# Chunk log sums by VectorE transposes instead of one-column matmuls in a fused gated-linear-attention and squared-ReLU kernel, with the last output tile evicted in halves

## The chip, the cores and the metric

The kernel runs on one core of one Trainium2 chip. The metric is device time in microseconds (us), the median of several runs. Engine names are those of the profile: PE is TensorE (PEld its weight loads), DVE is VectorE, ACT is ScalarE, POOL is GpSimd, SP is SyncE, which issues the DMAs.

## The reference

Two stages. The first is a recurrence over 768 steps for 4 batches x 8 heads with head size 48; its result is the input of a two-layer block with a squared ReLU.

```python
# q, k, v, alpha: (4, 8, 768, 48), alpha in 0.8 to 1.0
for t in range(S):
    state = alpha[:, :, t, :, None] * state + einsum('bhd,bhe->bhde', k[:, :, t], v[:, :, t])
    y[:, :, t] = einsum('bhd,bhde->bhe', q[:, :, t], state)
x = y.transpose(0, 2, 1, 3).reshape(3072, 384)
out = square(maximum(x @ w_in, 0)) @ w_out      # w_in 384 x 2048, w_out 2048 x 384
```

## The kernel before

**Chunks.** The 3072 tokens are 24 chunks of 128 tokens, six to a batch (`NCH = 6`). The recurrence is done chunk by chunk in matrix form. For a chunk, `at` (alpha) is loaded and ScalarE takes its logarithm into `L_s`. A step called `p0` on TensorE multiplies `L_s` by an upper triangle of ones (`utri_b`): its 384 columns are the cumulative log sums of all rows, in the PSUM bank `pm`. Four more matmuls of `p0`, one for each pair of heads, have `L_s` as weights and a single column of ones: they give the sum over the whole chunk with the head's channel on the partition, four columns more in the same bank. From `pm` ScalarE reads `A` = exp, `Ainv` = exp(-), and the two halves of `ae_s` = exp of the chunk sums (L421 to L431). VectorE makes `qA_s = q * A` (L440) and `kI_s = k * Ainv` (L443); TensorE transposes both (`p1q`, `p1k`), VectorE copies them out as `qkT` (L367), and so on: scores `sc`, masked scores `sm` (L504), the state update `st` (matmul, then VectorE's `st * ae_s`, L538, then ScalarE's copy `sb`), the chunk's output `py` (steps `p3a`, `p3b`), its copy `xn`, its transpose (`p4`) and the copy into `xT_big`. `p0`, `p1`, `p4` and others take one of two PSUM banks (`GLA_BANKS`) in turn. Chunks 0 to 3 are handled as two double chunks in another layout (`add_super`); from chunk 8 on, chunks go in pairs, so a pair has an even and an odd chunk. The ones-column form of `p0` serves every chunk from 4 to 23.

**The block.** `add_moe1` multiplies `xT_big` by `w_in` (three matmuls of 256 or 128 or 512 columns to a piece, then ScalarE's relu `r`, L790, and VectorE's square into `gT`, L798). `add_moe2` multiplies `gT` by `w_out` (16 matmuls of 384 columns to a token tile), ScalarE or VectorE copies the PSUM bank to `ob` (L828, L830), and SP issues one DMA of 192 KB to the output (L837).

**What sets the order.** All work is entered as `Op`s with an engine, a guessed duration, dependences and a priority. `Plan.run` is a list scheduler in Python: it places every op by these guesses, and then emits all ops in the order of their planned starts. The engines therefore run a written-out order; each engine works strictly in that order, and what the guesses miss becomes a wait on the chip. The guesses include `LD` (us for one load of a chunk's tensor, 1.05) and `OUT_LATE = 3.5` (an output DMA's planned start is that much later than its eviction). `gate` lets a chunk's `p0` start only when it is at most 3.5 chunks ahead of the block. The framework below adds the semaphore waits for data and for shared buffers, PSUM banks among them.

Of the kernel before, what the change touches and what calls it, by code (L numbers as in the profile page):

```python
# [8 lines left out]
FP32 = mybir.dt.float32  # L9
BF16 = mybir.dt.bfloat16  # L10
AF = mybir.ActivationFunctionType
# [45 lines left out]
def after(op, x=0.0):  # L57
    return (op, x)
# [86 lines left out]
def kernel(  # L145
# [10 lines left out]
    nc = tc.nc  # L156
    B, H, S, D = q.shape
    HD = H * D
    P = 128
    DP = 64  # L160
    NP = H // 2
    NCH = S // P
    d_model, d_ff = moe_w_in.shape
# [3 lines left out]
    NT = n_tok // P  # L167
# [5 lines left out]
    out_r = out.rearrange("(tt p) n -> tt p n", p=P)  # L173
# [73 lines left out]
    def pin(ins):  # L247
        tc.keep_in_program_order(ins)

    def mm(*a, **kw):  # L250
        pin(nc.tensor.matmul(*a, **kw))  # L251
# [14 lines left out]
    def psum(op, shape, dt):  # L266
        i = op.slot.bank
        return banks[i].tile(shape, dt, name=f"bank{i}")
    X_SLACK = 0.2
    LD = 1.05  # L270
    LD2 = 1.51
    WLD = 2.05
    SQ_PRIO = 0.0
# [1 line left out]
    def add(eng, dur, emit, *deps, **kw):  # L275
        return plan.add(Op(eng, dur, emit, deps, **kw))
# [46 lines left out]
    state = {}  # L323
    SRC = dict(srcs)
    EARLY = 2 * 3
    PAIRS = 8
    LEAD = 3.5

    NS = 2
    SIDE = 1  # L330
    EITHER, SLOW = {"DVE": 0.47, "POOL": 0.95}, {"POOL": 0.95}
    KI_ON = [[EITHER, EITHER], [EITHER, EITHER]]
# [59 lines left out]
    def add_chunk(s):  # L392
        d = C[s]
        b, c = divmod(s, NCH)
        i = s % NBUF
        L, qA, kI, ae = L_s[:, i], qA_s[:, i], kI_s[:, i], ae_s[:, i]
        old = C[s - NBUF].get("end") if s >= NBUF else None
        g = dict(prio=-10.0 + s * 0.01)
        last = c == NCH - 1

        def e_ln():
            pin(nc.scalar.activation(L[:, :, 0:D], d["at"], AF.Ln))  # L402
        ln = d["use_at"] = add("ACT", 0.41, e_ln, d["ld_at"], old, prio=-15.0 if s < EARLY else -5.0)

        def e_vb():
            d["vb"] = work.tile([P, H, D], BF16, name="vb", bufs=4)
            pin(nc.gpsimd.tensor_copy(d["vb"], d["vt"]))  # L407
        vb = d["use_vt"] = add("POOL", 0.55, e_vb, d["ld_vt"], old, prio=-5.0)

        def e_p0():  # L410
            pm = d["pm"] = psum(p0, [P, 512], FP32)
            mm(pm[:, 0:HD], lhsT=utri_b[:, 0, :], rhs=L[:, :, 0:D], start=True, stop=True)
            for p in range(NP):
                mm(pm[:, HD + p:HD + p + 1], lhsT=L[:, 2 * p:2 * p + 2, :], rhs=ones_col,
                   start=True, stop=True)
        p0 = Op("PE", 0.27, e_p0, [ln], takes=GLA_BANKS, lat=0.17, **g)
        p0.gla = s

        def e_A():
            d["A"] = work.tile([P, H, D], BF16, name="A")  # L420
            pin(nc.scalar.activation(d["A"], d["pm"][:, 0:HD].rearrange("p (h d) -> p h d", h=H), AF.Exp))  # L421

        def e_Ai():
            d["Ai"] = work.tile([P, H, D], BF16, name="Ainv")
            pin(nc.scalar.activation(d["Ai"], d["pm"][:, 0:HD].rearrange("p (h d) -> p h d", h=H), AF.Exp, scale=-1.0))  # L425

        def e_ae0():
            pin(nc.scalar.activation(ae[0:64, :, 0], d["pm"][0:64, HD:HD + NP], AF.Exp))

        def e_ae1():  # L430
            pin(nc.scalar.activation(ae[64:128, :, 1], d["pm"][64:128, HD:HD + NP], AF.Exp))  # L431
        plan.add(p0)
        a_ = add("ACT", 0.38, e_A, p0, **g)
        ai = add("ACT", 0.38, e_Ai, p0, after(a_), **g)
        ae0 = add("ACT", 0.18, e_ae0, p0, after(ai), **g)
        ae1 = add("ACT", 0.19, e_ae1, p0, after(ae0), **g)
        p0.gives = ae1

        def e_qA():
            pin(nc.vector.tensor_mul(qA[:, :, 0:D], d["qt"], d["A"]))  # L440

        def e_kI():
            pin(nc.vector.tensor_mul(kI[:, :, 0:D], d["kt"], d["Ai"]))  # L443
        mq = d["use_qt"] = add("DVE", 0.47, e_qA, a_, d["ld_qt"], old, **g)
        mk = d["use_kt"] = add("DVE", 0.47, e_kI, ai, d["ld_kt"], old, **g)

        def e_p1q():
            d["pT"] = psum(p1q, [P, 2 * NP, P], BF16)
            for p in range(NP):
                tr(d["pT"][:, p, :], qA[:, 2 * p:2 * p + 2, :], ident_bf)  # L450

        def e_p1k():
            for p in range(NP):
                tr(d["pT"][:, NP + p, :], kI[:, 2 * p:2 * p + 2, :], ident_bf)
        p1q = plan.add(Op("PE", 0.22, e_p1q, [mq], takes=GLA_BANKS, **g))
        p1k = plan.add(Op("PE", 0.22, e_p1k, [mk, after(p1q)], lat=0.15, **g))

        def e_cp(lo, hi):
            if lo == 0:
                d["qkT"] = work.tile([P, 2 * NP, P], BF16, name="qkT")  # L460
            cast(cpk if lo else cp, d["qkT"][:, lo:hi, :], d["pT"][:, lo:hi, :])
        if s < EARLY:
            cp = add({"ACT": 0.49, "DVE": 0.34}, 0, lambda: e_cp(0, NP), p1q, **g)
            cpk = add({"DVE": 0.34, "ACT": 0.49}, 0, lambda: e_cp(NP, 2 * NP), p1k, after(cp, -9.0), **g)
        else:
            cp = cpk = add("DVE", 0.61, lambda: e_cp(0, 2 * NP), p1k, **g)
        p1q.gives = cpk

        d.update(cps=[cp, cpk], mk=mk, vb_op=vb, ae1=ae1, kI=kI, ae=ae)
        if s < PAIRS:  # L470
            add_scores(s, 1)
            add_back(s)
        elif s % 2:
            add_scores(s - 1, 2)
            add_back(s - 1)
            add_back(s)
# [90 lines left out]
    def add_super(u):  # L567
# [135 lines left out]
        for ab in any_:  # L703
            s = 2 * u + ab
            c = pair[ab]
            r = slice(HF * ab, HF * ab + HF)
            before = C[s - 1].get("sb") if s else None
            if s < NCH - 1:
                def e_ps(c=c, r=r, s=s):
                    if s == 0:  # L710
                        state["ps"] = ps_st.tile([P, NP, 2 * D], FP32, name="st")
                    st = c["st"] = state["ps"]
                    for t in any_:
                        for p in range(NP):
                            mm(st[:, p, :], lhsT=kI[r, t, 2 * p:2 * p + 2, :], rhs=d["vb"][t][r, 2 * p:2 * p + 2, :],
                               start=(s == 0 and t == 0 and p == 0), stop=True, skip_group_check=True)
                ps = plan.add(Op("PE", 0.35, e_ps, [*mk, *vb, ae1, before], lat=0.16, **g))

                def e_stm(c=c, ab=ab):
                    st4 = c["st"].rearrange("p n (j e) -> p n j e", j=2)  # L720
                    pin(nc.vector.tensor_mul(st4, st4, bcast(ae[:, ab], D)))  # L721
                stm = add("DVE", 0.47, e_stm, ps, ae1, prio=ST_PRIO)

                def e_sb(c=c):
                    c["sbt"] = work.tile([P, NP, 2 * D], BF16, name="sb")
                    pin(nc.scalar.copy(c["sbt"], c["st"]))
                c["sb"] = add("ACT", 0.37, e_sb, stm, prio=-12.0)

            def e_p3a(c=c, r=r, s=s, ab=ab):
                c["py"] = psum(c["p3a"], [P, 512], FP32)  # L730
                for p in range(NP):
                    mm(c["py"][:, 2 * p * D:2 * (p + 1) * D], lhsT=d["qT"][:, p, ab].rearrange("k t c -> k (t c)"), rhs=C[s - 1]["sbt"][:, p, :],
                       start=(p == 0), stop=False, skip_group_check=True)

            def e_p3b(c=c, r=r, s=s):
                if s == 0:
                    c["py"] = psum(c["p3b"], [P, 512], FP32)
                for x in any_:
                    for hh in range(2):
                        for p in range(NP):  # L740
                            h = 2 * p + hh
                            mm(c["py"][:, h * D:(h + 1) * D], lhsT=d["sm"][x][r, hh, p, :], rhs=d["vb"][x][r, h, :],
                               start=(s == 0 and x == 0 and hh == 0 and p == 0), stop=(x == 1), skip_group_check=True)
            p3a = None
            if s:
                p3a = c["p3a"] = plan.add(Op("PE", 0.2, e_p3a, [cq, before], takes=SUP_BANKS, **g))
            p3b = c["p3b"] = plan.add(Op("PE", 0.5, e_p3b, [*sm, *vb, after(p3a)], takes=None if s else SUP_BANKS,
                                         lat=0.15, **g))
            add_tail(s, p3b, p3a or p3b, g)

    GN = [4, 1, 1, 2, 2, 2, 2, 2, 2, 2, 2, 2]
    assert sum(GN) == NT
# [52 lines left out]
    def add_moe2(g, tt, before, box, quarters, pools):  # L805

        for qd in quarters:
# [12 lines left out]
            op.lat = 0.05  # L820
            before = op
        if quarters[-1] < NQ - 1:
            return op

        def e_ev():
# [113 lines left out]
```

## Time and profile before

| | |
|---|---|
| time, median of 3 runs | 189.08 us (188.58 to 189.12) |
| the profiled execution: its own time, its span | 187.66 us, 185.9 us |
| PE busy | 178.4 us, 96% of the span, granted clock 0.999 |
| DVE busy | 133.8 us (72%) |
| ACT busy | 122.6 us (66%) |
| POOL busy | 29.6 us (16%) |
| DMA, all of it from SP's queue but instruction loads | 29.89 MB, mean 163 GB/s |
| matmuls with the column of ones | 80, 4.8 us of overlapping durations |
| `ae_s` from PSUM, ScalarE | 2 x 20, 172 and 170 ns each |

A matmul's duration in the trace contains its way through the array, so that the next one starts long before it ends: what TensorE spends on it is the distance between starts. The same holds, less strongly, for VectorE and ScalarE back to back. "Idle before" of a group is the time that its engine stood idle just ahead of it, and the engine named behind it is the one whose semaphore ended that.

### The profile page before, as it was taken

To read this page: it belongs to the slowest core of one execution; us is meant where nothing else is said; L and a number is where in the kernel's file an instruction comes from. 1 tells how busy PE (TensorE), PEld (TensorE's weight loads), DVE (VectorE), ACT (ScalarE), POOL (GpSimd) and SP (SyncE) were. 2 spreads that over 40 slices of the span, in tenths; PEclk is the share of its full clock that TensorE was granted. 3 is DMA by queue.
4 is the path that set the end of the run, shared out by engine and by line. 5 is a ranking of instruction groups with operands and counts; after the bars stand their busy time and mean duration, and the time that the engine had idled before them with its cause. 6 is when DMAs were issued, how large, how long until landed. Compare 5 with 4: busy or idle time off the path is not lost.

```text
span 185.9 us, 5105 instructions
## 1 busy us (share of the span) xinstructions
PE 178.4 (96%) x2037; PEld 134.1 (72%) x2037; DVE 133.8 (72%) x280; ACT 122.6 (66%) x282; POOL 29.6 (16%) x47
## 2 busy tenths in 40 slices
PE   6889899999999999999999999999999999999992
PEld 2666684667887878878878878777868778767761
DVE  7688679875999986876976966866987976842400
ACT  3577779455896896776676776667778668434621
POOL 5044777411012111111020020020020000000000
PEclk9999999999999999999999999999999999999999
DMA  5999999899899999999997984691011011011112
GB/s 146 261 280 339 385 370 331 175 223 205 161 206 209 236 199 231 184 231 201 189 222 162 216 166 101 157 212 61 0 42 46 2 48 42 4 42 42 46 43 84
DMA packets 99176, 30.22 MB, mean 163 GB/s; under 512 B 92112, under 2 KB 98000, under 8 KB 99152
## 3 DMA queue, kind: packets, MB, share of 16 engines
q1 hardware_dynamic: 99152, 29.89, 68.1%
q8 instruction: 16, 0.26, 0.5%
q14 instruction: 8, 0.07, 0.1%
HBM read 25.17 MB, written 4.72 MB: 161 GB/s over the span
## 4 chain that ended last, share of the span: by engine, by line
PE 88%; DMA 3%; ACT 3%; SPq 2%; DVE 1%; issue 0%
PE bank L251 77%; PE bank L254 7%; DMA at<-in_alpha_dram 3%; PE sc L251 2%; PE st L251 2%; SPq L360 2%; DVE qkT L367 1%; ACT raw L691 1%; ACT L_s L579 0%; DVE qA_s L627 0%; ACT w_in_b L304 0%; DVE st L721 0%; ACT r L790 0%; ACT ob L830 0%; ACT A L610 0%
## 5 line engine op out<-in xcount | busy, mean ns | idle before, releaser
L251 PE MATMUL bank<-xT_big,w_in_b 128*128 128x256 bf16 (+2 forms) x600 | 73.1, 269 | 0.0
L251 PE MATMUL bank<-w_out_b,gT 128*128 128x384 bf16 x384 | 72.4, 326 | 0.0
L790 ACT ACTIVATE r<-bank 128x512 bf16<-128x512 f32 x96 | 56.9, 602 | 18.8 <-PE bank L251 16.5
L251 PEld LDWEIGHTS <-w_in_b 128*128 128x128 bf16 x600 | 52.5, 98 | 9.2
L798 DVE TENSOR_TENSOR gT<-r 128x512 bf16<-128x512 bf16 x96 | 45.2, 493 | 17.1 <-ACT r L790 16.6
L251 PEld LDWEIGHTS <-gT 128*128 128x128 bf16 x384 | 35.1, 97 | 17.8
L407 POOL CAST vb<-vt 128x384 bf16<-128x384 f32 x20 | 10.9, 550 | 92.7 <-PE bank L251 45.6
L367 DVE COPY qkT<-bank 128x1024 bf16<-128x1024 bf16 (+1 forms) x26 | 16.5, 649 | 6.3 <-PE bank L254 6.2
L830 ACT COPY ob<-bank 128x384 f32<-128x384 f32 x20 | 9.6, 479 | 14.6 <-PE bank L251 14.6
L504 DVE TENSOR_TENSOR sm<-sc,utri_b 128x512 bf16<-128x512 f32 x24 | 15.4, 684 | 2.0 <-PE sc L251 2.0
L365 ACT CAST xn<-bank 128x384 bf16<-128x384 f32 x24 | 10.9, 481 | 5.8 <-PE bank L251 5.7
L440 DVE TENSOR_TENSOR qA_s<-qt,A 128x384 bf16<-128x384 f32 x20 | 11.5, 577 | 3.8 <-ACT A L421 3.7
L251 PEld LDWEIGHTS <-qkT 64*128 64x128 bf16 (+2 forms) x304 | 10.4, 98 | 4.9 <-issue 2.5
L421 ACT ACTIVATE A<-bank 128x384 bf16<-128x384 f32 x20 | 9.9, 494 | 6.2 <-PE bank L251 6.2
L367 DVE COPY xT_big<-bank 128x384 bf16<-128x384 bf16 x21 | 7.4, 354 | 8.3 <-PE bank L254 8.2
L443 DVE TENSOR_TENSOR kI_s<-kt,Ainv 128x384 bf16<-128x384 f32 x20 | 11.3, 567 | 0.0
L543 ACT CAST sb<-st 128x384 bf16<-128x384 f32 x16 | 7.6, 476 | 5.2 <-DVE st L538 5.2
L402 ACT ACTIVATE L_s<-at 128x384 bf16<-128x384 f32 x20 | 10.0, 520 | 0.5 <-DMA at<-in_alpha_dram 0.4
L504 DVE TENSOR_TENSOR sm<-bank,utri_b 128x512 bf16<-128x512 f32 x16 | 10.2, 681 | 0.0
L251 PE MATMUL bank<-warm 128*128 128x256 bf16 (+1 forms) x41 | 8.2, 333 | 2.0 <-DVE both L216 1.3
L425 ACT ACTIVATE Ainv<-bank 128x384 bf16<-128x384 f32 x20 | 9.9, 496 | 0.0
L251 PE MATMUL bank<-vb,sm 128*128 128x48 bf16 (+1 forms) x224 | 9.6, 183 | 0.0
(70 smaller groups left out, 176.3 us busy)
## 6 DMA issues: line engine op xcount, KB each, us to landing
at<-in_alpha_dram SPq DMA_DIRECT2D x20, 192.0 KB, 3.9
qt<-in_q_dram SPq DMA_DIRECT2D x20, 192.0 KB, 3.7
kt<-in_k_dram SPq DMA_DIRECT2D x20, 192.0 KB, 4.0
vt<-in_v_dram SPq DMA_DIRECT2D x20, 192.0 KB, 3.7
out_dram<-ob SPq DMA_DIRECT2D x20, 192.0 KB, 2.3
wo<-in_moe_w_out_dram SPq DMA_DIRECT2D x4, 768.0 KB, 6.8
wi<-in_moe_w_in_dram SPq DMA_DIRECT2D x3, 768.0 KB, 8.0
at<-in_alpha_dram SPq DMA_DIRECT2D x2, 384.0 KB, 4.9
```

The source lines that it names most:

```text
L251: pin(nc.tensor.matmul(*a, **kw))
L254: pin(nc.tensor.transpose(*a))
L365: pin(nc.scalar.copy(out_t, in_t))
L367: pin(nc.vector.tensor_copy(out_t, in_t))
L402: pin(nc.scalar.activation(L[:, :, 0:D], d["at"], AF.Ln))
L407: pin(nc.gpsimd.tensor_copy(d["vb"], d["vt"]))
L421: pin(nc.scalar.activation(d["A"], d["pm"][:, 0:HD].rearrange("p (h d) -> p h d", h=H), AF.Exp))
L440: pin(nc.vector.tensor_mul(qA[:, :, 0:D], d["qt"], d["A"]))
L443: pin(nc.vector.tensor_mul(kI[:, :, 0:D], d["kt"], d["Ai"]))
L504: pin(nc.vector.tensor_mul(d["sm"][:, hh], d["sc"][hh], utri_b.to_broadcast([P, NP, P])))
L790: pin(nc.scalar.activation(box["r"][:, 0:w], box["ph"][:, 0:w], AF.Relu))
L798: pin(nc.vector.tensor_mul(gT[g][:, f0:f0 + per, lo * P:lo * P + n], r, r))
```

## The change

- From chunk 12 on (`TURN = 12`), `p0` keeps its 384-column matmul and loses the four one-column ones. VectorE instead transposes, in 32 x 32 blocks, the last 32 rows of the cumulative sums (partitions 96 to 127 of `pm`, where row 127 holds the chunk's sums): two instructions for a chunk, for channels 0 to 31 and for 16 to 47 of each of the eight heads, into a tile `tot`. ScalarE's `ae_s` is then made by four small exponentials that read column 31 of the blocks in `tot`, instead of two that read `pm`. The bank is given back, in the planner, after `Ainv` and the second transpose.
- The last token tile's eviction is split: VectorE copies 192 columns and SP issues their DMA, ScalarE copies the other 192 and issues their DMA itself. This SP issue has no `OUT_LATE`.
- `LD`, the planner's guess for a load, goes from 1.05 to 0.97.
- In the double chunks, `p3b` of both chunks is entered after the loop over them, and chunk 0's PSUM bank is taken by a planner-only op. `JOIN` keeps one `p3b` to a chunk.

```diff
-    LD = 1.05
+    LD = 0.97
...
+    TURN = 12
...
+    JOIN = [[(0,), (1,)], [(0,), (1,)]]
...
             mm(pm[:, 0:HD], lhsT=utri_b[:, 0, :], rhs=L[:, :, 0:D], start=True, stop=True)
-            for p in range(NP):
+            for p in range(NP if s < TURN else 0):
                 mm(pm[:, HD + p:HD + p + 1], lhsT=L[:, 2 * p:2 * p + 2, :], rhs=ones_col,
                    start=True, stop=True)
-        p0 = Op("PE", 0.27, e_p0, [ln], takes=GLA_BANKS, lat=0.17, **g)
+        p0 = Op("PE", 0.27 if s < TURN else 0.17, e_p0, [ln], takes=GLA_BANKS, lat=0.17, **g)
...
-        ae0 = add("ACT", 0.18, e_ae0, p0, after(ai), **g)
-        ae1 = add("ACT", 0.19, e_ae1, p0, after(ae0), **g)
-        p0.gives = ae1
+        Q = P - 32
+
+        def e_turn(w):
+            if w == 0:
+                d["tot"] = work.tile([P, 2, H, 32], FP32, name="tot", bufs=2)
+            pm = d["pm"][Q:P, 32 * w:32 * w + 1]
+            src = bass.AP(tensor=pm.tensor, offset=pm.offset, ap=[pm.ap[0], [D, H], [0 if w else 16, 2], [1, 16]])
+            pin(nc.vector.transpose(d["tot"][Q:P, w], src))
+
+        def e_aet(j, w):
+            n = 16 if w else 32
+            o = HF * j + 32 * w
+            src = d["tot"][Q:Q + n, w, :, 31].rearrange("p (n a) -> p a n", a=2)[:, j]
+            pin(nc.scalar.activation(ae[o:o + n, :, j], src, AF.Exp))
+        if s < TURN:
+            ae0 = add("ACT", 0.18, e_ae0, p0, after(ai), **g)
+            ae1 = add("ACT", 0.19, e_ae1, p0, after(ae0), **g)
+            p0.gives = ae1
+        else:
+            turn = add("DVE", 0.34, lambda: e_turn(0), p0, **g)
+            turn = add("DVE", 0.34, lambda: e_turn(1), p0, after(turn), **g)
+            ae1 = ai
+            for j in range(2):
+                for w in range(2):
+                    ae1 = add("ACT", 0.18, lambda j=j, w=w: e_aet(j, w), turn, after(ae1), **g)
+            fin = add("NIL", 0.0, lambda: None, ai, turn, lat=0.0, **g)
+            p0.gives = fin
...
             if s:
-                p3a = c["p3a"] = plan.add(Op("PE", 0.2, e_p3a, [cq, before], takes=SUP_BANKS, **g))
-            p3b = c["p3b"] = plan.add(Op("PE", 0.5, e_p3b, [*sm, *vb, after(p3a)], takes=None if s else SUP_BANKS,
-                                         lat=0.15, **g))
-            add_tail(s, p3b, p3a or p3b, g)
+                c["hold"] = plan.add(Op("PE", 0.2, e_p3a, [cq, before], takes=SUP_BANKS, **g))
+            else:
+                c["hold"] = plan.add(Op("NIL", 0.0, e_hold, sm, takes=SUP_BANKS, lat=0.0, **g))
...
+        for abs_ in JOIN[u]:
+            p3b = plan.add(Op("PE", 0.5 + 0.1 * len(abs_) - 0.1, lambda abs_=abs_: e_p3b(abs_),
+                              [*sm, *vb, *[pair[ab]["hold"] for ab in abs_]], lat=0.15, **g))
+            for ab in abs_:
+                add_tail(2 * u + ab, p3b, pair[ab]["hold"], g)
...
+        half = d_model // 2
+        if GT[g] + tt == NT - 1:
+            def e_evh(i):
+                if "ob" not in box:
+                    box["ob"] = opool.tile([P, 2, half], FP32, name="ob2", tag="ob")
+                cast(evs[i], box["ob"][:, i], box["po"][:, i * half:(i + 1) * half])
+
+            def e_outh(i):
+                pin((nc.sync, nc.scalar)[i].dma_start(out=out_r[NT - 1, :, i * half:(i + 1) * half], in_=box["ob"][:, i]))
+            evs = []
+            for i, e in enumerate(("DVE", "ACT")):
+                evs.append(add(e, 0.28, lambda i=i: e_evh(i), op, prio=-15.0))
+            add("OUT", 0.3, lambda: e_outh(0), evs[0], at=0.0)
+            add("ACT", 0.3, lambda: e_outh(1), evs[1])
+            box["first"].gives = evs[1]
+            return op
```

More of the change, by code (lines that the diff above doesn't have):

```diff
@@ L729, in e_p3a @@
             def e_p3a(c=c, r=r, s=s, ab=ab):
-                c["py"] = psum(c["p3a"], [P, 512], FP32)
+                c["py"] = psum(c["hold"], [P, 512], FP32)
                 for p in range(NP):
@@ L733, in e_p3a, with e_hold, e_p3b @@
                        start=(p == 0), stop=False, skip_group_check=True)
[L735 to L744, printed above, removed]
-            if s:
-                p3a = c["p3a"] = plan.add(Op("PE", 0.2, e_p3a, [cq, before], takes=SUP_BANKS, **g))
-            p3b = c["p3b"] = plan.add(Op("PE", 0.5, e_p3b, [*sm, *vb, after(p3a)], takes=None if s else SUP_BANKS,
-                                         lat=0.15, **g))
-            add_tail(s, p3b, p3a or p3b, g)
+            def e_hold(c=c):
+                c["py"] = psum(c["hold"], [P, 512], FP32)
+            if s:
+                c["hold"] = plan.add(Op("PE", 0.2, e_p3a, [cq, before], takes=SUP_BANKS, **g))
+            else:
+                c["hold"] = plan.add(Op("NIL", 0.0, e_hold, sm, takes=SUP_BANKS, lat=0.0, **g))
+        def e_p3b(abs_):
+            for x in any_:
+                for hh in range(2):
+                    for p in range(NP):
+                        h = 2 * p + hh
+                        for ab in abs_:
+                            r = slice(HF * ab, HF * ab + HF)
+                            mm(pair[ab]["py"][:, h * D:(h + 1) * D], lhsT=d["sm"][x][r, hh, p, :],
+                               rhs=d["vb"][x][r, h, :], start=(2 * u + ab == 0 and x == 0 and hh == 0 and p == 0),
+                               stop=(x == 1), skip_group_check=True)
+        for abs_ in JOIN[u]:
+            p3b = plan.add(Op("PE", 0.5 + 0.1 * len(abs_) - 0.1, lambda abs_=abs_: e_p3b(abs_),
+                              [*sm, *vb, *[pair[ab]["hold"] for ab in abs_]], lat=0.15, **g))
+            for ab in abs_:
+                add_tail(2 * u + ab, p3b, pair[ab]["hold"], g)
     GN = [4, 1, 1, 2, 2, 2, 2, 2, 2, 2, 2, 2]
```

## The prediction, made before the changed kernel ran

> **What bounds the kernel now.** I read the page first, then the waits of TensorE, then the timeline around one `p0`, the last microseconds, and the start of VectorE's work.
>
> The page's head and its slices:
>
> ```profile
> span 185.9 us, 5105 instructions
> ...
> PE 178.4 (96%) x2037; PEld 134.1 (72%) x2037; DVE 133.8 (72%) x280; ACT 122.6 (66%) x282; POOL 29.6 (16%) x47
> ...
> PE   6889899999999999999999999999999999999992
> DVE  7688679875999986876976966866987976842400
> ```
>
> TensorE is full from 20 us to 182 us. Its waits (engine waited for: us, times, longest) come to 4 us in all, and all lie in the first 20 us:
>
> ```profile
> PE bank L251 <- ACT L_s L579: 1.4, 2, 1.0
> PE bank L251 <- DVE both L216: 1.3, 1, 1.3
> PE bank L251 <- ACT r L790: 0.8, 1, 0.8
> ```
>
> So a matmul taken out is time won, and a new wait of TensorE is time lost, at full price: its order is fixed and nothing later is idle to take it up. The timeline around the `p0` of an even chunk (start us, us):
>
> ```profile
> 95.86 0.33 PE L251 MATMUL bank<-L_s,utri_b 128*128 128x384 bf16 x1
> 96.03 0.24 PE L251 MATMUL bank<-ones_col,L_s 128*128 128x1 bf16 x4
> 96.13 0.81 PE L251 MATMUL bank<-w_out_b,gT 128*128 128x384 bf16 x4
> 96.30 0.49 ACT L421 ACTIVATE A<-bank 128x384 bf16<-128x384 f32 x1 [0.57 <-PE bank L251]
> 96.69 0.49 ACT L425 ACTIVATE Ainv<-bank 128x384 bf16<-128x384 f32 x1
> 96.78 0.33 PE L254 MATMUL bank<-ident_bf,xn 128*128 128x128 bf16 x3
> 96.83 0.56 DVE L440 TENSOR_TENSOR qA_s<-qt,A 128x384 bf16<-128x384 f32 x1 [0.40 <-ACT A L421]
> 96.94 1.46 PE L251 MATMUL bank<-w_out_b,gT 128*128 128x384 bf16 x8
> 97.30 0.55 DVE L443 TENSOR_TENSOR kI_s<-kt,Ainv 128x384 bf16<-128x384 f32 x1
> 98.24 0.39 PE L254 MATMUL bank<-ident_bf,qA_s 128*128 128x128 bf16 x4
> 98.47 0.39 PE L254 MATMUL bank<-ident_bf,kI_s 128*128 128x128 bf16 x4
> ```
>
> Two things are to be seen. The four one-column matmuls hold TensorE from 96.03 to 96.13, 0.10 us. And the chain `p0`, `A`, `qA_s`, `kI_s` ends 0.6 to 0.9 us before TensorE comes to transpose it: `qA_s` ends at 97.39 for 98.24, `kI_s` at 97.85 for 98.47. That slack is what hides the chain.
>
> **The matmuls removed.** Chunks 12 to 23: 12 x 0.10 = 1.2 us off TensorE, on the path. The Trainium skill ("TensorE: Matmul & The Clock Gate", section on LDWEIGHTS) gives a weight load of 128 columns as 128/1.2 = 107 ns; if loads set the pace, an estimate from that page would be 48 x 0.107 = 5.1 us off in place of 1.2, and the forecast 3.9 us lower. By that rule four would take 0.43 us; the trace has 0.10 and disagrees.
>
> **The transposes added: a wait between two engines.** What the planner enters is two VectorE steps that start with `A`. What the built program has is another thing; its order with the semaphores shows it. In every even chunk: `A` waits for PE, the first transpose for ScalarE's count that `A` brings, `Ainv` for VectorE's count of the first transpose, the second transpose for `Ainv`. On VectorE's queue the lines stand as
>
> ```
> StreamTranspose tot 32x256 [waits Activation] x2
> TensorTensor qA_s<-qt,A
> TensorTensor kI_s<-kt,Ainv
> ```
>
> All four read one PSUM bank, and readers on different engines are put one behind the other. `qA_s` needs only `A`, but stands behind the second transpose in an in-order queue, so it now waits for `Ainv` too. Before, all readers were ScalarE's. The Trainium skill says the same against this change ("PSUM — Partial Sum Buffer", section "PSUM bank collisions raise a hardware error"): two engines must not be in the same bank and 32 partitions at once, ScalarE and VectorE reads included. No run here shows two at once.
>
> Price of one transpose (32 x 256 floats from PSUM): no row has one. The copy of 384 floats takes 558 ns (L828), the masked product of 512 takes 681 ns: 0.12 per 128, so 0.43 for 256. Nearest rows for the ends: 0.35 (`xT_big` copy, 354 ns) and 0.56. I take 0.43. A hop from one engine to the next is 0.04 (`A` ends 96.79, `qA_s` starts 96.83). At a change of start partition VectorE doesn't overlap two instructions; the masks show it, where the fifth starts at partition 64:
>
> ```profile
> 4.12 0.18 DVE L226 CAST mask_E<-utri_f 64x64 bf16<-64x64 f32 x1
> 4.23 0.18 DVE L227 CAST mask_O<-utri_f 64x64 bf16<-64x64 f32 x1
> 4.42 0.19 DVE L226 CAST mask_E<-utri_f 64x64 bf16<-64x64 f32 x1
> ```
>
> 0.19 apart against 0.10. So the transposes, at partition 96, count in full.
>
> *Even chunk*, us from the start of `p0`: `A` 0.44 to 0.93 (as before), transpose 0.97 to 1.40, `Ainv` 1.44 to 1.93, transpose 1.97 to 2.40, `qA_s` 2.41 to 2.97, `kI_s` (0.47 behind it, as now) 2.88 to 3.43. TensorE reaches the `qA_s` transposes after `p0`, 4 + 8 `w_out` matmuls and 3 transposes: 0.17 + 0.65 + 0.16 + 1.30 = 2.28. It waits until 3.01 (0.73), does four (0.22), and waits from 3.23 to 3.47 for `kI_s` (0.24): 0.97.
>
> *Odd chunk*: here the first transpose comes ahead of `A`, `A` waits for it, the second transpose for `A`, `Ainv` for that. VectorE is free only when the even chunk's `st` ends, 1.59 after the `kI_s` transposes start (98.47 to 99.50 + 0.56); the odd `p0` starts 0.22 + 0.17 + 0.65 = 1.04 after them, so the transpose runs 0.56 to 0.99 of the odd `p0`; `A` 1.03 to 1.52; transpose 1.56 to 1.99; one square (0.34 apart) to 2.34; `qA_s` to 2.90. TensorE arrives at 0.17 + 3 x 0.65 + 0.33 = 2.45: 0.49 lost. Behind it a square, an eviction and `kI_s` end at 4.18, for TensorE's 3.65 + 0.49: 0.08. Together 0.57.
>
> A pair loses 1.54; six pairs 9.2 us. Ends: transposes of 0.35 take 0.16 off each chunk (7.3 us), of 0.56 add 0.26 (12.3 us); with the odd chunks hidden altogether, 5.8.
>
> **What lies beside it.** ScalarE has 24 more `ae_s` (0.17 each, 4.1 us) and is busy 52.5 of the 75 us from 82 to 157; they end near 3.1 for an `st` product past 4.4: nothing. If that cover went, `sb` and the next `p3a` would be late. Relus behind `Ainv` lose at most its 0.5 us of waiting, as TensorE does: nothing more. The bank is free at 2.40, not 1.54, but its taker, the `qA_s` transposes, waits for `qA_s` anyway. VectorE gets 24 x 0.43 = 10.3 us and three more whole evictions (0.56) in a stretch where it is busy 57.5 of 75: under the 84 it would last. Below nothing: none of these can gain, as TensorE had no wait there.
>
> **The end.** Now: last matmul out at 182.53, eviction 0.48, issue at 183.03, landing 1.86 later (issue 0.33, then SP's wait of 1.5 for the landing), 1.0 to the end of the span. After: VectorE's half takes 558 less 1.5 x 0.12 = 0.37, ScalarE's 0.29. But the order of SP's queue has the half ahead of the whole DMA of the tile before, which keeps its `OUT_LATE` and so now stands last. SP issues the half at 0.40 and that tile at 0.78, landing at 2.64, where the last landing was 2.37: +0.3. With the three transfers in each other's way up to +0.9; without the exchange of places -0.1.
>
> **LD and the double chunks.** Before 60 us the order of `p0` and scores moves by a few places; nothing is removed. TensorE's small gaps from 50 to 70 us could close (-0.5); or ScalarE's `L_s` could wait for a load, since DMA engines are full there (share 1.02 and 1.06) and `p0` goes earlier (+0.8). In the double chunk, `p3a` changes places with `p3b` inside a stretch that waits for `qA_s`. I take 0.
>
> **Sum.** -1.2 + 9.2 + 0.3 = +8.3 us. The profiled execution took 187.66 (185.9 of span and 1.8 around it), so 196.0 with a span of 194.2; the median shown is 1.4 above that execution, so 197.4 for the median.
>
> **Rivals.**
> 1. *The waits aren't where I put them: faster.* If the four readers overlap (the counts waited for are met before `A` and `Ainv` end), the chain has two transposes more on VectorE at most beside `A`, `kI_s` would end near 2.3, inside 2.28 + 0.22, and only the removal stays: -1.2 + 0.3 = -0.9, 188.2. It decides when `qA_s` ends by 2.24. Against: the chain as built would need transposes of 0.07 us. For: only that no trace shows this wait yet. 0.05.
> 2. *The transposes are far slower.* At 1.0 us each the chain grows by 1.14 a chunk: 12 x 1.14 = 13.7 more, 211. VectorE itself would become the bound at 1.2 us each: a pair lasts 14.0 (95.86 to the next even `p0` at 109.83) and would last 15.5, VectorE's work in it is 57.5 / 75 x 14.0 = 10.7, and there are four. No row near is above 0.69. 0.05.
> 3. *Half hidden.* Odd chunks lose nothing and transposes take 0.35: 6 x (0.97 - 0.16) = 4.9, less 0.9 is +4.0, 193.1; for it speaks that the odd sum hangs on one VectorE position. 0.08.
>
> **How the numbers follow.** The forecast gets 0.82. Its range: 7.3 - 0.9 = +6.4 (195.5) to 12.3 - 0.9 = +11.4 (200.5). I go down to 193.0 for rival 3 and up to 200.5; the far ends of 1 and 2 are left out. 0.3% (0.57 us) is about what a measurement of this kernel can tell from no change. Faster 0.04 (most of rival 1), same 0.03, slower 0.93.
>
> **What would show it.** In the trace after: no matmul with `ones_col` past 80 us, 24 transposes near 430 ns; TensorE idle some 0.7 us before the `qA_s` transposes of chunks 12, 14 and so on, released by `qA_s`; `Ainv` starting not 0.39 but about 1.0 after `A`; VectorE idle ahead of the second transpose, released by `Ainv`; a whole output DMA issued last. It is wrong if TensorE's slices stay at 9 without waits for `qA_s` past 80 us.

## The result and the profile after

The changed kernel takes 200.41 us (median of 6 runs, 198.67 to 200.77), the kernel before 188.81 us beside it (6 runs): a ratio of 1.0605, 95% interval 1.0554 to 1.0655. It is slower by 11.6 us, where 8.3 were forecast. The forecast of 197.4 us was 3.0 too low; the time lies just inside the range, whose upper end was 200.5.

The page of the profiled execution (200.77 us), its head and TensorE's slices:

```profile
span 199.0 us, 5049 instructions
...
PE 184.0 (92%) x1988; PEld 132.7 (67%) x1989; DVE 144.5 (73%) x309; ACT 128.7 (65%) x302; POOL 29.6 (15%) x47
...
PE   6999889999999999989998998998998998999991
```

The row of nines now has an 8 in every third slice or so from the eighteenth on, where chunk 12 begins. The waits (engine, line, what it waited for: us in all, times, longest) name the place:

```profile
DVE tot L444 <- ACT A L423: 5.6, 12, 0.6
PE bank L254 <- DVE qA_s L466: 5.6, 12, 0.6
...
PEld L254 <- DVE kI_s L469: 3.4, 13, 0.3
DVE tot L444 <- ACT Ainv L427: 3.3, 6, 0.6
ACT Ainv L427 <- DVE tot L444: 3.1, 6, 0.5
```

Each of the twelve chunks makes TensorE wait for `qA_s` once. VectorE's transposes (`tot`) wait for ScalarE's exponentials, and these for the transposes: the two engines take turns at one bank. None of the four needs anything from another, for all of them only read the bank; the waits are the semaphores that the framework adds for a shared bank. The timeline from the `p0` of chunk 14 (start us, duration us, engine, line, operation) shows the turns:

```profile
101.83 0.33 PE L251 MATMUL bank<-L_s,utri_b 128*128 128x384 bf16 x1
...
102.23 0.50 ACT L423 ACTIVATE A<-bank 128x384 bf16<-128x384 f32 x1
...
102.76 0.46 DVE L444 STREAM_TRANSPOSE tot<-bank 32x256 f32<-32x256 f32 x1 [0.38 <-ACT A L423]
...
103.25 0.49 ACT L427 ACTIVATE Ainv<-bank 128x384 bf16<-128x384 f32 x1 [0.52 <-DVE tot L444]
...
103.78 0.46 DVE L444 STREAM_TRANSPOSE tot<-bank 32x256 f32<-32x256 f32 x1 [0.56 <-ACT Ainv L427]
104.26 0.56 DVE L466 TENSOR_TENSOR qA_s<-qt,A 128x384 bf16<-128x384 f32 x1
...
104.88 0.40 PE L254 MATMUL bank<-ident_bf,qA_s 128*128 128x128 bf16 x4 [0.61 <-DVE qA_s L466]
...
105.35 0.40 PE L254 MATMUL bank<-ident_bf,kI_s 128*128 128x128 bf16 x4
```

No two of the four readers overlap, and `qA_s`, which needs only `A` (ended at 102.73), starts at 104.26 behind the second transpose. Before, the `qA_s` transposes came 2.38 us after `p0` without a wait; now 3.05.

The two profiled executions, cut at TensorE's landmarks (starts of the first `w_in` matmul, the first and the last `w_out` matmul, us):

| stretch | before | after | difference |
|---|---|---|---|
| start to first `w_in` | 17.85 | 19.47 | +1.62 |
| to first `w_out` | 14.57 | 15.66 | +1.09 |
| first to last `w_out` (the middle) | 149.75 | 159.51 | +9.76 |
| to the end of the span | 3.75 | 4.41 | +0.66 |

The middle holds all chunks from 4 on, and the last row is the tail. The first two rows lie ahead of every transpose, and differ from execution to execution: the run without transposes (below) has the same order on TensorE, ScalarE and VectorE up to 86 us, and comes to its first `w_out` matmul at 33.39 us, the changed kernel at 35.13. Of the second row 0.83 us is one wait of the changed kernel, which that run doesn't have:

```profile
26.17 0.34 PE L254 MATMUL bank<-ident_bf,xn 128*128 128x128 bf16 x3 [0.83 <-ACT xn L367]
```

To the first row the last experiment comes back. The two rows make the profiled difference (13.1) larger than that of the medians (11.6), and below the middle is given for each kernel, since it doesn't contain them.

### The profile page after: what moved, and what is told of

Read it like the earlier page. It is cut to its first block, busy times and chain, and to the rows that moved or that the text cites. A ratio compares the mean times of both kernels' runs of the same rounds, so it can differ in the third digit from the quotient of the medians.

```text
span 199.0 us, 5049 instructions
## 1 busy us (share of the span) xinstructions
PE 184.0 (92%) x1988; PEld 132.7 (67%) x1989; DVE 144.5 (73%) x309; ACT 128.7 (65%) x302; POOL 29.6 (15%) x47
## 4 chain that ended last, share of the span: by engine, by line
PE 67%; DVE 15%; ACT 10%; issue 4%; DMA 2%; DVEq 0%
PE bank L251 56%; PE bank L254 7%; DVE tot L444 6%; DVE qA_s L466 3%; ACT A L423 3%; PE sc L251 2%; ACT Ainv L427 2%; DMA at<-in_alpha_dram 2%; DVE st L564 2%; ACT ob L880 2%; DVE qkT L369 2%; DVE kI_s L469 1%; PE st L251 1%; ACT r L823 1%; DVE gT L831 1%
## 5 line engine op out<-in xcount | busy, mean ns | idle before, releaser
L251 PE MATMUL bank<-w_out_b,gT 128*128 128x384 bf16 x384 | 71.4, 326 | 0.0
L823 ACT ACTIVATE r<-bank 128x512 bf16<-128x512 f32 x96 | 56.3, 600 | 17.8 <-PE bank L251 16.1
L251 PEld LDWEIGHTS <-w_in_b 128*128 128x128 bf16 x600 | 52.7, 98 | 10.6 <-issue 0.4
L831 DVE TENSOR_TENSOR gT<-r 128x512 bf16<-128x512 bf16 x96 | 44.1, 483 | 9.5 <-ACT r L823 8.9
L251 PEld LDWEIGHTS <-gT 128*128 128x128 bf16 x384 | 35.7, 98 | 19.0
L409 POOL CAST vb<-vt 128x384 bf16<-128x384 f32 x20 | 10.2, 518 | 101.8 <-PE bank L251 37.3
L444 DVE STREAM_TRANSPOSE tot<-bank 32x256 f32<-32x256 f32 x24 | 10.9, 456 | 9.1 <-ACT A L423 5.6
L369 DVE COPY xT_big<-bank 128x384 bf16<-128x384 bf16 x22 | 7.8, 355 | 10.4 <-PE bank L254 10.2
L880 ACT COPY ob<-bank 128x384 f32<-128x384 f32 x16 | 7.7, 478 | 11.5 <-PE bank L251 11.3
L254 PE MATMUL bank<-ident_bf,qA_s 128*128 128x128 bf16 x96 | 9.5, 228 | 5.6 <-DVE qA_s L466 5.6
L254 PEld LDWEIGHTS <-qA_s 128*128 128x128 bf16 x96 | 6.5, 102 | 10.3 <-DVE qA_s L466 9.6
L251 PEld LDWEIGHTS <-qkT 64*128 64x128 bf16 (+2 forms) x304 | 10.2, 97 | 4.6 <-issue 1.8
L251 PE MATMUL bank<-warm 128*128 128x256 bf16 (+1 forms) x41 | 9.5, 379 | 2.0 <-DVE both L216 1.3
```

The lines of the kernel that those rows point to most:

```text
L254: pin(nc.tensor.transpose(*a))
L369: pin(nc.vector.tensor_copy(out_t, in_t))
L444: pin(nc.vector.transpose(d["tot"][Q:P, w], src))
L823: pin(nc.scalar.activation(box["r"][:, 0:w], box["ph"][:, 0:w], AF.Relu))
L831: pin(nc.vector.tensor_mul(gT[g][:, f0:f0 + per, lo * P:lo * P + n], r, r))
L880: pin(nc.scalar.copy(box["ob"], box["po"]))
```

## The experiments

All were timed in five rounds against the kernel before on the same chip; ratios are to it, with a 95% interval. Kernels of different rounds are compared by their ratios, at 188.6 us to the whole, and by their middles.

**The place of the transposes.** The changed kernel with the first transpose depending on `Ainv` too, so that both come when ScalarE has done with the two big reads:

```diff
-            turn = add("DVE", 0.34, lambda: e_turn(0), p0, **g)
+            turn = add("DVE", 0.34, lambda: e_turn(0), p0, ai, **g)
```

> The changed kernel with one more dependence in the planner: the transposes of a chunk come behind Ainv, so that A and Ainv read the bank one after the other on ScalarE as before, and VectorE's two reads follow. Same instructions, another order. If the alternation of the two engines on one bank is the cost (theory 1), TensorE's waits for qA_s past 80 us (0.77 and 0.49 us for an even and an odd chunk in the changed kernel's trace) go, and what may stay is kI_s behind two transposes, up to 0.3 us a chunk: 188.5 to 192 us. If the transposes' own time on VectorE is the cost (rival: 24 x 0.456 = 10.9 us of VectorE), nothing changes: 199 to 201 us.

Measured: 191.56 us, ratio 1.0196 (1.0144 to 1.0249), middle 151.71. One more dependence takes back 7.7 us by the ratios (0.0605 less 0.0196) and 7.8 by the middles. Its VectorE timeline at chunk 14:

```profile
100.11 0.55 DVE L466 TENSOR_TENSOR qA_s<-qt,A 128x384 bf16<-128x384 f32 x1
100.69 0.80 DVE L444 STREAM_TRANSPOSE tot<-bank 32x256 f32<-32x256 f32 x2
101.52 0.56 DVE L469 TENSOR_TENSOR kI_s<-kt,Ainv 128x384 bf16<-128x384 f32 x1
```

The transposes run back to back without a wait between them, and `qA_s` stands ahead of them. The same instructions are there as in the changed kernel, in another order: the dependence moved other work too (TensorE now has `w_in` matmuls ahead of its transposes of `qA_s` and between these and those of `kI_s`). Most of the loss was in the order, not in the instructions.

**Everything but the transposes.** `TURN = 24`: no chunk transposes, all keep the one-column matmuls; `LD`, the entry of `p3b` and the halves stay.

> The changed kernel with TURN = 24: no transposes, all 20 ones-column groups kept; LD, the entry of p3b and the halves of the last eviction stay. It gives the price of the rest alone. Theory 1: the transposes cost 10.6 us of waits less 1.2 us of matmuls, so this one is 9.4 us under the changed kernel: 190 to 191.5 us, 1 to 2 us over the kernel before (0.3 to 0.7 at the end, the rest from LD's order before 80 us). Rival (LD or the start carries a good part): 193 us or more.

Measured: 190.81 us, ratio 1.0133 (1.0093 to 1.0172), middle 151.32. The transposes, less what they replace, cost 8.9 us (0.0605 less 0.0133; 8.2 by the middles); the rest of the change costs 2.5, for which the forecast had 0.3.

**What the matmuls are worth.** Also without the one-column matmuls from chunk 12 on, and without transposes.

> As the one before, but from chunk 12 on the one-column matmuls are left out as well, and ScalarE's two exponentials read four columns of the cumulative sums in place of the chunk sums (so the chunk decay is not computed there). It prices the 48 matmuls alone. By the distance of starts (0.10 us for four) 1.2 to 1.3 us under the kernel without transposes; if weight loads of 97 ns set the pace, 4 to 5 us under it.

Measured: 189.42 us, ratio 1.0056 (1.0029 to 1.0084), middle 148.71: by the medians 1.4 us under the run before it. The forecast had 1.2. By the middles it is 2.6, of which 0.79 is a wait of the run before that this one doesn't have (68.41 us, shown further down).

**The transposes without the bank.** The changed kernel, with the transposes reading a constant tile in SBUF in place of the PSUM bank; all these instructions stay, and TensorE, ScalarE and VectorE have them in the same order.

```diff
-            pm = d["pm"][Q:P, 32 * w:32 * w + 1]
+            pm = flat[Q:P, 32 * w:32 * w + 1]
```

> The changed kernel with the transposes in the same place of VectorE's queue, but reading a constant tile in SBUF in place of the PSUM bank (so the chunk decay is not computed from chunk 12 on). VectorE keeps its 24 instructions, ScalarE its 48; only the shared bank is gone. Theory 1 (bank): the waits go, and the time is that of the kernel without matmuls and transposes within 1 us: 188.5 to 191. Rival (VectorE's time or its queue): within 2 us of the changed kernel, 198 or more.

Measured: 189.17 us, ratio 1.0065 (1.0026 to 1.0103), middle 149.25. The 24 transposes are still there, 0.42 us each, and the kernel is 10.2 us faster than the changed one (0.0605 less 0.0065; by the middles 10.3) and no slower than the run that has none of them (by the middles 0.5 us slower). Its timeline of VectorE at an even chunk:

```profile
127.79 0.77 DVE L446 STREAM_TRANSPOSE tot<-flat 32x256 f32<-32x256 f32 x2
128.59 0.56 DVE L468 TENSOR_TENSOR qA_s<-qt,A 128x384 bf16<-128x384 f32 x1
```

The two run in time in which VectorE had nothing to do, and past 80 us TensorE has no wait left. So 10 us of VectorE work cost about half a microsecond at most in this place, and the sharing of one bank between VectorE and ScalarE cost as much as all the waits in the chunks: the two theories are told apart. The reordered kernel above, which still reads the bank, is 2.5 us slower than this one; which part of its other order costs that isn't shown.

**The three smaller edits, each alone on the kernel before.** First `LD = 0.97`:

> The kernel before with LD = 0.97 and nothing else of the change. The run without transposes was 2.4 us above the kernel before although it has 1.4 us less of matmuls than this one only if the ones matmuls are counted; so the remainder of the change (LD, the entry of p3b in the double chunks, the halves of the last eviction) costs about 2.4 us, of which the tail shows 0.7. Theory A: LD moves p0 of the early chunks and carries most of what remains: 189.5 to 190.3. Theory B: LD is worth nothing, as the prediction had it, and the remainder is the entry of p3b or start-up: 188.2 to 188.7.

Measured: 190.12 us, ratio 1.0049 (1.0018 to 1.0079), middle 151.19 (+1.44). The medians are 1.4 us apart, the ratio gives 0.9, with an interval of 0.3 to 1.5. More than half of what the middle gained is one wait:

```profile
76.10 0.52 ACT L402 ACTIVATE L_s<-at 128x384 bf16<-128x384 f32 x1 [1.25 <-DMA at<-in_alpha_dram]
...
77.16 0.60 PE L251 MATMUL bank<-xT_big,w_in_b 128*128 128x256 bf16 x4 [0.82 <-ACT r L790]
```

The planner, told that loads are quicker, has put this `L_s` ahead of the `A` that it followed before; the load lands late, ScalarE stands for 1.25 us, and the relu behind it holds TensorE for 0.82. The first theory holds for `LD` alone. In the whole change the wait comes and goes. The run without transposes has it:

```profile
68.41 0.49 PE L251 MATMUL bank<-xT_big,w_in_b 128*128 128x256 bf16 x3 [0.79 <-ACT r L823]
```

The changed kernel, with the same order up to there, hasn't: in its profile the load is 0.38 us late at this place, and TensorE doesn't wait.

Then the last eviction in halves:

> The kernel before with the last eviction in two halves and nothing else. Theory A: the halves read one PSUM bank, are put one behind the other, and the tile before is issued last on SP: +0.6 to +0.7, 189.0 to 189.2, with the second half starting where the first ends. Theory B (the prediction's): the halves run side by side, +0.3, 188.7.

Measured: 189.23 us, ratio 1.0027 (1.0006 to 1.0047), and from the start of the first copy of the last tile to the end of the span 4.05 us, for 3.39 before: the +0.66 of the first theory. In the changed kernel's tail (`ACTq` and `SPq` are the DMA issues of ScalarE and SP):

```profile
195.00 0.32 ACT L367 COPY ob<-bank 128x192 f32<-128x192 f32 x1 [2.12 <-PE bank L251]
195.35 0.37 ACTq L866 DMA_DIRECT2D out_dram<-ob  x1
195.35 0.36 DVE L369 COPY ob<-bank 128x192 f32<-128x192 f32 x1 [7.10 <-ACT ob L367]
195.74 0.33 SPq L866 DMA_DIRECT2D out_dram<-ob  x1
196.16 0.41 SPq L887 DMA_DIRECT2D out_dram<-ob  x1
```

VectorE's half waits for ScalarE's: they read one bank, so the halves take 0.71 us together and not 0.36, and the whole DMA of the tile before goes out last (195.00 + 1.16); SP's wait for its landing ends at 198.10. (They also write one tile, `ob`. That this is the reason isn't likely: in the kernel before VectorE writes the tile `kI_s` from 13.60 to 14.16 us, and GpSimd another part of it from 14.07, released by ScalarE and not by VectorE.)

And the entry of `p3b`:

> The kernel before with only the other entry of p3a and p3b in the two double chunks (JOIN, hold). Theory A: the run without transposes was 2.1 us above before; the halves alone cost 0.5 and LD alone 1.4, so nearly nothing is left for this part: 188.5 to 189.1. Theory B: it moves the early xn and so the first w_out matmul, which in the changed kernel came about 1 us later than the start explains: 189.5 to 190.

Measured: 190.67 us, ratio 1.0108 (1.0072 to 1.0144). The first theory fails, and the second gives a cause that isn't there: from the first `w_in` to the first `w_out` matmul it takes 14.65 us, 14.57 before. In its profile half is in the middle (150.79, +1.04: the chunks' places shift and small waits appear near 69 and 71 us), half in a start that is 1.0 later. The three alone add to 0.9 + 0.5 + 2.0 = 3.5 us, together they cost 2.5. The difference is within the intervals of the four ratios. The profiles point the same way: the middles gain 1.44, 0.33 and 1.04, and together 1.57. Each edit makes the planner write out another order, so there is no reason for them to add up.

**Can the matmuls be replaced at a profit?** The kernel before, only with the transposes, behind `Ainv` and at low priority:

```diff
+            turn = add("DVE", 0.44, lambda: e_turn(0), ai, prio=-5.0)
+            turn = add("DVE", 0.44, lambda: e_turn(1), ai, after(turn), prio=-5.0)
```

> The kernel before with the transposes from chunk 12 on, entered behind Ainv and at a lower priority so that they stand behind qA_s and kI_s in VectorE's queue; LD, the entry of p3b and the last eviction stay as before. Theory A (the loss is the place in the chain of the bank's readers): TensorE has no wait for qA_s, 1.2 to 1.4 us of matmuls are gone, less what remains of small waits: 187.0 to 188.4. Theory B (VectorE's time itself costs, about 11 us more of it): above 190.

Measured: 189.48 us, ratio 1.0044 (1.0018 to 1.007), middle 151.37, against the first theory, and short of the second's 190. No matmul waits for `qA_s` any more, but VectorE now has 0.87 us more between `kI_s` and its next work, and comes late elsewhere:

```profile
122.53 1.28 DVE L529 TENSOR_TENSOR sm<-bank,utri_b 128x512 bf16<-128x512 f32 x2
...
123.27 0.33 PE L251 MATMUL bank<-sb,qkT 128*128 128x96 bf16 x4 [0.33 <-DVE sm L529]
```

By the distances between TensorE's starts, such waits and stretched distances take 2.2 us more from 80 us on than in the kernel before: more than the matmuls gave.

The same with the last rows copied to SBUF by ScalarE:

```diff
+            pin(nc.scalar.copy(d["low"][Q:P], d["pm"][Q:P, 0:HD]))
...
-            pm = d["pm"][Q:P, 32 * w:32 * w + 1]
+            pm = d["low"][Q:P, 32 * w:32 * w + 1]
```

> As c1, but ScalarE, the engine that reads the bank anyway, copies the last 32 rows of the sum to SBUF (32 x 384 floats, one more activation a chunk), and VectorE transposes that copy. Theory A (only the sharing of the bank between engines costs): 187.0 to 188.2, at or under c1. Theory B (ScalarE's longer chain holds up the relus or ae): 188.5 to 190.

Measured: 191.58 us, ratio 1.013 (1.0089 to 1.017), middle 151.97, above the ranges of both theories. ScalarE is busy 133.6 us for 122.6. Relus, `ae_s` and `sm` together are about 10% of the chain that ended last, where the kernel before has 0% of relus and none of the others. But the run before this one has the same share without the copy, so that ScalarE's lateness is what this one adds is argued, not shown.

The last row of `A`, which lies in SBUF, is already the exponential of the chunk's log sum. Four transposes of its last 32 rows need neither the bank nor an exponential:

```diff
+            A = d["A"][Q:P, j, 32 * w:32 * w + 1]
...
+            pin(nc.vector.transpose(aeT[o:o + 32, i, :, j], src))
```

> The kernel before, from chunk 12 on without the four ones matmuls and without any new reader of the bank: A holds the exponentials in SBUF, so its last row is already exp of the chunk's log sum; VectorE transposes rows 96 to 127 of A (bf16, four transposes of 32x128) straight to the rows where ae is read, behind qA_s at low priority, and ScalarE's two small exps go. The decay is then rounded to bf16. Theory A (the loss was the sharing of the bank plus the longer work on ScalarE and VectorE behind it): 187.2 to 188.4, that is the 1.4 us of matmuls less some small waits. Theory B (VectorE's added time behind kI_s costs as much as it did in c1, because gT and sm come later): 189 to 190.

> As d1, with the transposes at the chunk's usual priority, so that in many chunks they stand right behind qA_s and ahead of later gT products. Theory A: as d1, 187.2 to 188.4. Theory B: kI_s or gT pushed back by the four transposes; 189 to 190.5, above d1.

Measured: 191.41 us, ratio 1.015 (1.0112 to 1.0188), middle 152.93; and 192.7 us, ratio 1.0207 (1.0169 to 1.0245), middle 153.24. Both go the way of the second theory, and above its figures. A transpose of 32 x 128 takes 305 ns, four of them 1.22 us to a chunk behind `qA_s`. Here ScalarE does less than before (120.9 us busy for 122.6 in the first of the two), and these transposes are 4% of the chain that ended last: it points to VectorE's time at that place, though no run changes this alone. The one-column matmuls at 0.10 us to a chunk are cheaper than any of the four replacements.

**The start.** Nine dummy matmuls in place of seven ahead of the first product:

```diff
-    for _ in range(7):
+    for _ in range(9):
```

> The kernel before with nine dummy matmuls of 512 columns at the start in place of seven, so that TensorE's idle microsecond ahead of the first product of L_s is filled; nothing else. In the profiles so far the program starts in one of two ways: TensorE at full rate from 5.4 us (before, halves alone, c1, c3, d1) or at half rate until about 9 us, with everything behind it some 1.1 us later (the changed kernel, the others); the profiled run of before had the earlier one. Theory A: which of the two is a matter of how long TensorE is busy ahead of the first product, so the filled gap gives the early one always: median 187.6 to 188.2, with the spread of the runs cut. Theory B: it is chance, or set by something else: median within 0.3 of before and the same spread.

Measured: 187.91 us, ratio 0.995 (0.9923 to 0.9976); its 12 runs lie between 187.57 and 188.49, the 17 of the kernel before beside it between 187.91 and 190.18. The median and the spread are those of the first theory. The gain lies in how often the early start comes, and is read from the times: the one profile of this kernel (span 186.3 us) is no faster than the one profile of the kernel before (185.9), which had the early start too. TensorE's first product in this kernel, the group at 1.26 being the nine:

```profile
1.26 3.73 PE L251 MATMUL bank<-warm 128*128 128x512 bf16 x9 [1.26 <-DVE both L216]
5.58 0.32 PE L251 MATMUL bank<-L_s,half_in 128*128 128x384 bf16 x1 [0.59 <-ACT L_s L579]
```

and in the changed kernel:

```profile
5.40 0.48 PE L251 MATMUL bank<-L_s,half_in 128*128 128x384 bf16 x1 [0.98 <-ACT L_s L605]
```

The same product takes 0.32 us in the one and 0.48 in the other, which stays at half rate until about 10 us: the twelve dummy matmuls of 256 columns that follow take 1.47 us in the one and 2.72 in the other. The profile's granted clock reads 1.00 in this stretch in both, so only the matmuls show it. This is the one version here that beats both kernels, by half a percent; it owes nothing to the change.

## Why the prediction was right, and where its sizes were off

**The bound and the mechanism: right.** TensorE has no idle time to hide a wait, and the four readers of one bank alternate, as the built order said. The even chunk went by the clock of the forecast, from the start of `p0`:

| | forecast | measured |
|---|---|---|
| `A` | 0.44 | 0.40 |
| first transpose | 0.97 | 0.93 |
| `Ainv` | 1.44 | 1.42 |
| second transpose | 1.97 | 1.95 |
| `qA_s` | 2.41 | 2.43 |
| TensorE's transposes of `qA_s` | 3.01 | 3.05 |
| lost ahead of `qA_s`, of `kI_s` | 0.73, 0.24 | 0.77, 0.24 |

The losses are the distances between starts of TensorE's matmuls beyond the usual ones. A transpose took 0.456 us for 0.43.

**The odd chunk: order right, a quarter short.** Its first transpose came 0.57 us after `p0` (forecast 0.56), and 0.49 was lost ahead of `qA_s`, as forecast. Ahead of `kI_s` it was 0.17 for 0.08, and 0.09 was lost earlier, in the `w_in` matmuls behind `p0`: 0.75 for 0.57. The lines of chunk 15:

```profile
106.41 0.33 PE L251 MATMUL bank<-L_s,utri_b 128*128 128x384 bf16 x1
106.57 1.56 PE L251 MATMUL bank<-xT_big,w_in_b 128*128 128x256 bf16 x12
106.98 0.46 DVE L444 STREAM_TRANSPOSE tot<-bank 32x256 f32<-32x256 f32 x1
107.97 0.81 PE L251 MATMUL bank<-w_out_b,gT 128*128 128x384 bf16 x4
108.62 0.49 PE L251 MATMUL bank<-xT_big,w_in_b 128*128 128x256 bf16 x3
109.43 0.40 PE L254 MATMUL bank<-ident_bf,qA_s 128*128 128x128 bf16 x4 [0.32 <-DVE qA_s L466]
109.67 1.15 PE L251 MATMUL bank<-xT_big,w_in_b 128*128 128x256 bf16 x9
110.82 0.40 PE L254 MATMUL bank<-ident_bf,kI_s 128*128 128x128 bf16 x4
```

A pair so loses 1.76 for 1.54, six pairs 10.6 for 9.2.

**The matmuls: right.** 1.2 in the sum, 1.4 between two runs, and 1.8 between their middles without the wait of 0.79 us. The rival pace of 107 ns a weight load, 5.1 us, is excluded. In the kernel before, the four loads of one `p0` take 0.31 us from 95.86 on, while the 384-column matmul ahead of them runs; what they and their matmuls hold TensorE for is 0.10.

**The turns at the bank: they decided.** The transposes of SBUF were 10.2 us faster in the same order. By the Trainium skill ("PSUM — Partial Sum Buffer", section "PSUM bank collisions raise a hardware error") accesses of ScalarE and VectorE to one bank and 32 partitions must not coincide, reads included. The traces fit it: in the even chunk above each of the first three readers ends 0.03 or 0.04 us ahead of the next, and the halves of the last tile stand 0.03 apart; no two overlap. That is the work of the program's semaphores, so it doesn't test the rule: what two at once would do was not tried.

**The tail: mis-sized, 0.3 for 0.66.** The forecast issued SP's half at 0.40 us after the last matmul; it was issued at 0.74. It saw four readers of a bank taking turns in the chunks and forgot that the two halves are two readers of one bank as well. The exchange on SP's queue was right.

**"I take 0" for `LD` and the double chunks: the step that failed.** The rest of the change without the transposes costs 2.5 us; less the tail's 0.7 that is 1.8, where the forecast had bounds of -0.5 and +0.8 and took none. For `LD` the upper bound's mechanism is what happened in the run of `LD` alone and in the run without transposes, with its size (0.82 and 0.79 for 0.8), though not in the profile of the changed kernel. For the entry of `p3b`, "inside a stretch that waits for `qA_s`" was no cover: the edit rewrites the order beyond that stretch.

So +1.4 in the chunks, +0.4 in the tail, +1.8 in the rest, -0.2 in the matmuls and -0.3 for the kernel before, which measured 188.81 here for 189.08: together 3.1 for the 3.0 missing; the 1.8 carries an interval of 0.8 either way. Rivals 1 and 3 wanted at most 4.9 us of waits; rival 2 wanted transposes of 1 us.

**Some luck.** The upper end of the range was worked out from transposes of 0.56 us. They took 0.456; what brought the time up to that end were the terms above. Against the kernel before as measured beside it, +11.6 us is more than the +11.4 from which that end came.

**What stays open.** How much of the price of `LD` and of `p3b` alone is the late start: it shows in the profile of each, and a timed run doesn't tell which start it had. Whether these kernels have it oftener than the kernel before, and why, isn't known. Nor is how the 1.8 us divide in the changed kernel itself, in whose profile the wait for the late load is missing and another, at 26.17 us, stands.

## What to carry to other kernels

In a program built like this one, a second engine that reads a PSUM bank joins the line of its readers, and in an in-order queue all that stands behind it waits too: cost the chain of all readers, not the instruction. The same happened here where the work on one bank was split over two engines to be quicker. And where TensorE is full, a 0.1 us piece on it can still be cheaper than 0.9 us on an engine that is a quarter idle, unless that work falls just where this engine waits.

## What the runs showed of the hardware

- Two copies of 128 x 192 from one bank by two engines stand one after the other here: 0.36 behind 0.32 us, starts 0.35 apart, 0.71 together. One engine's copy of all 384 columns took 0.48.
- A 32 x 256 float transpose on VectorE takes 456 ns alone from PSUM; two in a row take 434 ns each (median) from PSUM and 421 from SBUF, with starts 0.37 to 0.39 us apart. A 32 x 128 bf16 one still takes 305 ns.
- What TensorE does ahead of its first product can decide a microsecond of the whole run. With seven dummy matmuls and an idle gap of 0.9 to 1.2 us behind them, the program started at full rate in five profiles (gaps of 0.98 to 1.11 us) and at half rate until 9 or 10 us in eight (0.89 to 1.15), so the length of the gap doesn't tell them apart; with nine and a gap of 0.6 it started at full rate in the one profile, and all twelve runs lie within 0.9 us. The longer work and the shorter gap weren't tried apart. By the Trainium skill ("TensorE: Matmul & The Clock Gate", section "Part 1: The HAM clock gate") full rate comes after about 3.4 us of sustained work, watched in a window that doesn't start with the kernel. The traces fit that: seven dummy matmuls last 3.17 us and may miss it, nine last 3.73.
